# A causal convolution and its experts: from two groups of four batches to four interleaved groups of two

## The chip, the cores and the metric

The kernel runs on one core of one Trainium2 chip. The metric is device time in microseconds (us) of one execution. A profiled execution is a further one, taken by the hardware profiler; times of single instructions come from it.

## What is computed

The reference convolves each of 8 batches (5696 positions, 128 channels) causally with a filter `h`, and sends each of the 45,568 resulting rows to one of 8 experts:

```python
Yf = np.fft.rfft(x, n=2 * S, axis=1) * np.fft.rfft(h, n=2 * S, axis=0)[None]
x = np.fft.irfft(Yf, n=2 * S, axis=1)[:, :S, :].reshape(B * S, D)
logits = x @ w_gate + modality_bias[modality_id]
e_idx = np.argmax(logits, axis=1)                   # gate_w: its softmax value
for e in range(8):
    mask = e_idx == e
    out[mask] = gate_w[mask, None] * (np.maximum(x[mask] @ w1[e], 0.0) @ w2[e])
```

`w1[e]` is 128 by 1024 and `w2[e]` is 1024 by 128, in float32.

## The kernel before

The transform is done as matrix products in stages, for a group `g` of four batches, side by side in the free dimension (512 columns).

- **`stage1(g)`** (L154 to L190): 45 steps `q`. Each loads 128 rows of `x`, splits them into a high part (ACT, L173) and a low part (DVE, L174), runs matmuls of the three products high·high, high·low, low·high (L179), and stores two results `z` to DRAM. Group 0 carries the filter's 128 columns too (640 in all). This splitting in two fp32r parts is used throughout the kernel; a plain fp32 matmul is one instruction in the code and two in the trace.
- **`stage23(g)`** (L195 to L290): 64 steps `k`. Each loads a slice of `z`, does two fp32 matmuls into `px` (L263), two products with the filter on DVE (L265), a sum of the two on POOL (L274; where `whole` holds, half on DVE, L271, and half on POOL, L272), the splitting (ACT L280, DVE L233) and the backward matmuls into `pu` (L243 to L245; plain fp32 in L241 where `whole`), and stores `ut` (ACT L246, then SP).
- **`stage4(g)`** (L306 to L432): again 45 steps `q`. Each loads `u`, splits it (ACT L339, DVE L340), finishes the transform (PE L346), transposes (L353) and computes logits (L360, or in bfloat16 pieces L372). After three `q` a chunk of some twenty small DVE operations picks the expert and a row number for every token, and POOL scatters the rows to DRAM into a region of their expert, 128 rows to an indirect DMA (`dispatch`, L301).
- **`Moe`** (L496 to L632): tiles of rows of one expert. A tile loads 512 rows (L511) and, where the expert changes, 1 MB of weights (L519, SP), splits the weights in four pieces (ACT L524, DVE L526), transposes the rows (L533), and takes eight steps `f` of three matmuls up (`gemm1`, L550 to L552), ReLU and splitting (ACT L555, DVE L556), and three matmuls down two steps later (`gemm2`, L572 to L574). `finish` transposes back (L585), scales (DVE L588) and scatters with four indirect DMAs (POOL L591). The tiles come in four levels, as soon as enough rows are routed: 18, 18 and 45 tiles of 512 rows, and 23 of 256 rows with four steps each.

The order of work: `stage1(0)` alone; then `stage23(0)` with `stage1(1)`; then `stage23(1)` with the first 27 steps of `stage4(0)`; then the experts, beside the other 18 steps of `stage4(0)` and all of `stage4(1)`. `run_all` interleaves such generators at fixed rates, and a scheduler then fixes the order of each engine's queue, which the engines run strictly in order. PSUM has eight banks of 512 fp32 columns: in the third stretch three for `px`, two for `pu`, two for `py` and one for the logits; beside the experts `ps4` has two, the logits one, `pxt` (rows transposed in and out) one, `ph` two and `po` two.

## Time and profile before

| | |
|---|---|
| time, median of 3 runs (lowest to highest) | 2391.52 us (2383.88 to 2395.12) |
| the profiled execution | 2400.92 us, its span 2399.1 us |
| mean granted TensorE clock in it | 0.931 |
| PE (matmuls) busy | 2107.9 us, 88% |
| DVE busy | 1759.2 us, 73% |
| ACT busy | 1418.6 us, 59% |
| POOL busy | 1223.6 us, 51% |
| DMA | 357.46 MB, 149 GB/s on average |

PE is TensorE, DVE VectorE, ACT ScalarE, POOL GpSimd and SP SyncE. The profiled execution is 9.4 us above the median of the runs, so a sum made from its rows is carried to a run by taking 9 us off. A busy PE is not PE at its peak: matmuls overlap, and a matmul at half the granted clock is busy twice as long, so work done is counted from starts, not from busy time.

### The profile page before, as it was taken

To read this page: it belongs to the slowest core of one execution; us is meant where nothing else is said; L and a number is where in the kernel's file an instruction comes from. 1 tells how busy PE (TensorE), PEld (TensorE's weight loads), DVE (VectorE), ACT (ScalarE), POOL (GpSimd) and SP (SyncE) were. 2 spreads that over 40 slices of the span, in tenths; PEclk is the share of its full clock that TensorE was granted. 3 is DMA by queue.
4 is the path that set the end of the run, shared out by engine and by line. 5 is a ranking of instruction groups with operands and counts; after the bars stand their busy time and mean duration, and the time that the engine had idled before them with its cause. 6 is when DMAs were issued, how large, how long until landed. Compare 5 with 4: busy or idle time off the path is not lost. (4 is left out here: it accounts for less than half of the span.)

```text
span 2399.1 us, 33712 instructions
## 1 busy us (share of the span) xinstructions
PE 2107.9 (88%) x9752; PEld 1549.5 (65%) x9752; DVE 1759.2 (73%) x2651; ACT 1418.6 (59%) x2560; POOL 1223.6 (51%) x1012
## 2 busy tenths in 40 slices
PE   6788988999889968896877876999999999999897
PEld 5655544445555436674756654688888888888896
DVE  6569999999879956683555644777777777777675
ACT  6657776555545446573655543566666666666675
POOL 2135455655877875525566655533333333333675
PEclk9999999999888878897888977999999999999999
DMA  9989998786767755332334421223112121112421
GB/s 336 334 301 308 303 293 260 228 270 213 214 197 216 215 155 165 97 127 78 110 110 132 133 78 45 84 80 116 44 43 79 45 80 44 44 45 73 137 75 53
DMA packets 195433, 357.46 MB, mean 149 GB/s; under 512 B 32437, under 2 KB 63513, under 8 KB 191408
## 3 DMA queue, kind: packets, MB, share of 16 engines
q1 hardware_dynamic: 150560, 270.52, 35.4%
q0 software_dynamic: 23520, 47.61, 5.9%
q10 hardware_dynamic: 21168, 37.17, 5.2%
q8 instruction: 78, 1.28, 0.2%
q14 instruction: 107, 0.88, 0.1%
HBM read 276.51 MB, written 157.43 MB: 181 GB/s over the span
## 5 line engine op out<-in xcount | busy, mean ns | idle before, releaser
L556 DVE SCALAR_TENSOR_TENSOR hl<-ph,hh 128x512 fp32r<-128x512 f32 x740 | 509.1, 689 | 325.5 <-ACT hh L555 264.6
L555 ACT ACTIVATE hh<-ph 128x512 fp32r<-128x512 f32 x740 | 444.0, 601 | 443.4 <-PE ph L552 346.8
L591 POOL DMA_INDIRECT out<-of,mrt x370 | 393.9, 1065 | 599.2 <-DVE of L588 470.5
L301 POOL DMA_INDIRECT rows<-rt,idx x360 | 404.7, 1124 | 182.5 <-issue 94.2
L572 PE MATMUL po<-hh,slot 128*128 128x512 f32 (+1 forms) x832 | 331.9, 399 | 41.6 <-issue 25.3
L550 PE MATMUL ph<-mxh,slot 128*128 128x512 f32 (+1 forms) x832 | 327.5, 394 | 19.1 <-DVE hl L556 14.7
L274 POOL TENSOR_TENSOR t<-t,t 96x1024 f32<-96x1024 f32 x90 | 251.9, 2806 | 162.8 <-DVE t L265 142.3
L552 PE MATMUL ph<-mxh,slot 128*128 128x512 f32 (+1 forms) x832 | 315.4, 380 | 1.6 <-issue 0.8
L573 PE MATMUL po<-hl,slot 128*128 128x512 f32 (+1 forms) x832 | 314.2, 378 | 0.1
L551 PE MATMUL ph<-mxl,slot 128*128 128x512 f32 (+1 forms) x832 | 314.3, 378 | 0.0
L574 PE MATMUL po<-hh,slot 128*128 128x512 f32 (+1 forms) x832 | 313.8, 377 | 0.0
L265 DVE TENSOR_TENSOR t<-px,hs 96x1024 f32<-96x1024 f32 x256 | 302.8, 1209 | 13.5 <-PE px L263 6.0
L263 PE MATMUL px<-z,m 96*96 96x512 f32 x512 | 275.9, 632 | 25.9 <-DVE t L265 22.2
L526 DVE TENSOR_TENSOR slot<-raw,slot 128x512 fp32r<-128x512 f32 x370 | 265.4, 720 | 10.9 <-ACT slot L524 10.0
L524 ACT CAST slot<-raw 128x512 fp32r<-128x512 f32 x416 | 251.7, 614 | 11.8 <-DMA raw<-in_w 11.8
L572 PEld LDWEIGHTS po<-hh,slot 128*128 128x128 f32 x832 | 160.4, 193 | 73.0 <-issue 29.0
L550 PEld LDWEIGHTS ph<-mxh,slot 128*128 128x128 f32 x832 | 161.5, 194 | 51.5 <-DVE hl L556 23.9
L246 ACT COPY ut<-pu 90x512 f32<-90x512 f32 x256 | 144.5, 582 | 80.0 <-PE pu L245 27.4
L340 DVE TENSOR_TENSOR ul<-u,uh 128x1024 fp32r<-128x1024 f32 x90 | 117.3, 1304 | 97.6 <-ACT uh L339 75.1
L552 PEld LDWEIGHTS ph<-mxh,slot 128*128 128x128 f32 x832 | 160.6, 193 | 33.6 <-issue 1.4
L573 PEld LDWEIGHTS po<-hl,slot 128*128 128x128 f32 x832 | 160.5, 193 | 31.8 <-issue 1.2
L574 PEld LDWEIGHTS po<-hh,slot 128*128 128x128 f32 x832 | 160.5, 193 | 30.3
(155 smaller groups left out, 3639.7 us busy)
## 6 DMA issues: line engine op xcount, KB each, us to landing
raw<-in_w SPq DMA_DIRECT2D x104, 1024.0 KB
z<-z SPq DMA_DIRECT2D x256, 180.0 KB
z<-z SPq DMA_DIRECT2D x90, 320.0 KB
z<-z SPq DMA_DIRECT2D x90, 256.0 KB
ua<-ut SPq DMA_DIRECT2D x128, 180.0 KB
ub<-ut SPq DMA_DIRECT2D x128, 180.0 KB
mrt<-rows SPq DMA_DIRECT2D x81, 260.0 KB
u<-ua ACTq DMA_DIRECT2D x63, 256.0 KB
```

Of the source, the lines that this page charges most:

```text
L263: nc.tensor.matmul(px[:KP], mm, zbuf[i][k % NZ], start=True, stop=True)
L265: nc.vector.tensor_tensor(prod[i].rearrange("p j (b d) -> p j b d", d=D), px[:KP].rearrange("p (b d) -> p b d", d=D).unsqueeze(1).to_broad ...
L301: nc.gpsimd.indirect_dma_start(views[count[0] % NVIEW], bass.IndirectOffsetOnAxis(ap=idx[:, t:t + 1], axis=0), rt[:, t, :], None, bounds_c ...
L550: nc.tensor.matmul(po, w[:, 0, 0, fs], st["xh"], start=True, stop=False)
L551: nc.tensor.matmul(po, w[:, 0, 0, fs], st["xl"], start=False, stop=False)
L552: nc.tensor.matmul(po, w[:, 0, 1, fs], st["xh"], start=False, stop=True)
L555: st["act"] = nc.scalar.activation(hh, ph, AF.Relu)
L556: nc.vector.scalar_tensor_tensor(hl, ph, 0.0, hh.bitcast(F32), op0=ALU.max, op1=ALU.subtract)
L572: nc.tensor.matmul(po, w[:, 1, 0, fs], hh[:, cs], start=k == 0, stop=False)
L573: nc.tensor.matmul(po, w[:, 1, 0, fs], hl[:, cs], start=False, stop=False)
L574: nc.tensor.matmul(po, w[:, 1, 1, fs], hh[:, cs], start=False, stop=k == 7)
L591: nc.gpsimd.indirect_dma_start(oviews[(t * NSUB + c) % NVIEW], bass.IndirectOffsetOnAxis(ap=ri[:, c, D + 1:D + 2], axis=0), of[:, c, :], N ...
```

## The change

The batches are taken in four groups of two. A group's tiles are 256 columns wide, and where two results stood in two banks, they now share one (`[128, 2, 256]`), so most copies to SBUF keep 512 columns. Counts of the parts that are done per group double: 4 x 45 steps of `stage1` and of `stage4` and 4 x 64 of `stage23`, each of half the width; `stage4` does two `q` together where it copies. Other edits:

- The order of work: `stage1` of group 0 alone; `stage23(0)` with `stage1(1)`; `stage23(1)` with `stage4(0)` and `stage1(2)`; then the experts, beside `stage4(1)` to `stage4(3)`, `stage23(2)`, `stage23(3)` and `stage1(3)`, at the rates `R4`, `R2` and `R1`. There are five levels: 14, 22, 22 and 23 tiles of 512 rows and 23 of 256.
- A `ring` of four PSUM banks (tile name `pb`) serves `stage1`, `px` and `pu` of the later groups, `stage4` and the experts' transposes. `po` has one bank instead of two; at step 2 of a tile no `gemm2` stands, at step 3 two.
- `stage23` splits every `k`; the sum `t` is on POOL (L285), for group 1 at even `k` on DVE. The logits are plain fp32 throughout.
- Stores of `z` (but for group 0) and of `ut` are issued by ACT; loads of `u` by SP.
- Weights are loaded in halves of 512 KB into one buffer each, less far ahead, and compared with the tile before (it was the tile before that); rows are loaded two tiles ahead (it was three).
- The bias goes through DRAM, the twiddle tables are loaded anew by every group, and the filter is reloaded with its negated third part.

The diff, cut to its core:

```diff
-NG = 2
+NG = 4
...
+LAG = 2
+R4 = {1: 0.95, 2: 0.55, 3: 0.6}
+R2, R1 = 0.6, 0.42
+DEPTH = 2
...
-    live = [[g, float(r), 0.0] for g, r in gens]
+    live = [[g, r if callable(r) else lambda r=r: r, 0.0] for g, r in gens]
     while live:
         for it in list(live):
-            it[2] += it[1]
+            it[2] += it[1]()
...
+            for g in range(NG):
+                nc.sync.dma_start(bd[g].rearrange("p (q b) e -> p q b e", b=GB),
+                                  bias.rearrange("p (q b) e -> p q b e", b=B)[:, :, g * GB:(g + 1) * GB])
...
+    def transform(g, q, ft, xx, ps, w):
+
+        for t in range(2):
+            for i, (a, b) in enumerate(((0, 0), (0, 1), (1, 0))):
+                nc.tensor.matmul(ps[:, t, :w], ft[:, a, 2 * t:2 * t + 2, :], xx[:, b], start=i == 0, stop=i == 2)
...
+                ps = ring.tile([128, 2, GC], F32, name="pb")
+                transform(g, q, ft[:, j], xx[:, :, j], ps, GC)
+                z = sp.tile([128, 2, GC], F32, name="z")
+                nc.scalar.copy(z, ps)
+                nc.scalar.dma_start(zd[g][2 * q:2 * q + 2].rearrange("e k t c -> (e k) (t c)"), z.rearrange("p t c -> p (t c)"))
+                yield
+        done.add((1, g))
...
+            pu = ring.tile([128, 2, GC], F32, name="pb")
+            for i in range(2):
+                nc.tensor.matmul(pu[:KP, i], mi[:, i, 0, :], yh[:, i], start=True, stop=False)
+                nc.tensor.matmul(pu[:KP, i], mi[:, i, 0, :], yl[:, i], start=False, stop=False)
+                nc.tensor.matmul(pu[:KP, i], mi[:, i, 1, :], yh[:, i], start=False, stop=True)
+            ut = sp.tile([90, 2, GC], F32, name="ut")
+            nc.scalar.copy(ut, pu[:90])
+            nc.scalar.dma_start(ud[g][:, k], ut)
...
-                px = psx.tile([128, 512], F32, name="px")
-                prod[i] = sp.tile([KP, 2, GC], F32, name=f"t{i}", bufs=4 if i else 5)
-                nc.tensor.matmul(px[:KP], mm, zbuf[i][k % NZ], start=True, stop=True)
+            px = pxp[0].tile([128, 2, GC], F32, name="pb")
+            for h, mm in ((0, m2), (1, m1)):
+                nc.tensor.matmul(px[:KP, h], mm, zbuf[k % NZ][:, 1 - h], start=True, stop=True)
+
+            yv = sp.tile([KP, 2, 2, GC], F32, name="t", bufs=3)
...
-            whole = (g == 1 or k >= W0) and k % WH == WH - 1
-            if whole:
-                nc.vector.tensor_tensor(y[:, 0], y[:, 0], prod[1][:, 0], op=ALU.add)
-                add = nc.gpsimd.tensor_tensor(y[:, 1], y[:, 1], prod[1][:, 1], op=ALU.add)
-            else:
-                add = nc.gpsimd.tensor_tensor(y, y, prod[1], op=ALU.add)
-            with tc.issue_after(add.ins):
-                dispatch(PACE)
-            yh = None
-            if not whole:
-                yh = sp.tile([KP, 2, GC], F32R, name="yh", bufs=4)
-                nc.scalar.copy(yh, y)
+            eng = nc.vector if dve_sum and k % dve_sum == 0 else nc.gpsimd
+            eng.tensor_tensor(yv[:, 0], yv[:, 0], yv[:, 1], op=ALU.add)
+            yh = sp.tile([KP, 2, GC], F32R, name="yh", bufs=3)
+            nc.scalar.copy(yh, yv[:, 0])
...
-            self.raw = [wp.tile([128, 2, FF], F32, name=f"raw{i}") for i in range(NSLOT)]
-            self.slots = [wp.tile([128, 2, 2, FF], F32R, name=f"slot{i}") for i in range(3)]
+        def __init__(self, wp, sp, psh, pso):
+            self.sp, self.psh, self.pso = sp, psh, pso
...
-            nc.sync.dma_start(self.raw[t % NSLOT], w12_d[bass.ds(ex, 1)].rearrange("o p a f -> (o p) a f"), cond=ch > 0)
+            nc.sync.dma_start(self.raw[i], w12_d[bass.ds(ex, 1), :, i].rearrange("o p f -> (o p) f"), cond=ch > 0)
...
-            steps = []
+            for t in range(DEPTH):
+                self.load(t)
+            self.load_weights(0, 0)
+            self.load_weights(0, 1)
+            for k in range(4):
+                self.split(0, k)
+            self.load_weights(1, 0)
...
+                    if f == 0:
+                        while not self.ready(t + DEPTH):
+                            yield
+                        self.load(t + DEPTH)
+                        self.load_weights(t + 1, 1)
+                    if f == n // 2:
+                        self.load_weights(t + 2, 0)
                     self.gemm1(t, f)
-                if g >= LAG:
-                    self.gemm2(*steps[g - LAG][:2])
-                if t + 1 < total:
-                    if n == 4 or f % 2 == 1:
-                        with tc.issue_after(self.st[t]["act"].ins):
-                            self.split(t + 1, f * 4 // n)
-                    if f == (4 if n == 8 else 1):
-                        self.prep(t + 1)
-                if f == LAG and t >= 1:
-                    self.finish(t - 1)
+                    due.append((t, f))
+                    if f == 3 and t >= 1:
+                        self.finish(t - 1)
+
+                    for _ in range(0 if f == 2 else 2 if f == 3 else len(due) > LAG):
+                        self.gemm2(*due.pop(0))
+                    if t + 1 < total:
+                        if n == 4 or f % 2 == 1:
+                            with tc.issue_after(self.st[t]["act"].ins):
+                                self.split(t + 1, f * 4 // n)
+                        if f == (4 if n == 8 else 1):
+                            self.prep(t + 1)
+                    yield
...
+    ring = ctx.enter_context(tc.tile_pool(name="ring", bufs=4, space=PSUM))
+    psl = ctx.enter_context(tc.tile_pool(name="psl", bufs=1, space=PSUM))
...
+            run_all((stage23(0, sp2, pxp, 0, hzp), 1), (stage1(1, sp1), 0.7))
...
+        run_all((stage23(1, sp2, pxp, 2), 1), (stage4(0, sp4, plt), 1.3), (stage1(2, sp1), 0.7), (pace(), 1))
...
+        pxp[0] = ring
...
+        def routing():
+            for g in range(1, NG):
+                rate["4"] = R4[g]
+                while (2, g) not in done:
+                    yield
+                yield from stage4(g, sp4, plt)
+                if g < NG - 1:
+                    fence()
+                    level(g, views[NVIEW])
...
+        def transforms():
+            for g in range(2, NG):
+                while (1, g) not in done:
+                    yield
+                yield from stage23(g, sp2, pxp)
+
+        def pace():
+            while "routing" not in done:
+                dispatch(1)
+                yield
+        run_all((routing(), lambda: rate.get("4", 1)), (transforms(), R2), (stage1(3, sp1), R1), (pace(), 1), (moe.run(), 1))
```

Where instructions now stand. The first place is on PE in the stretch where experts and transforms run together. Before, between `gemm1` (`ph`) and `gemm2` (`po`) steps stand matmuls of `stage4`, here six for one `q` (`py`):

```order
L346 MATMUL py<-uh,gt 128x512
L346 MATMUL py<-ul,gt 128x512
L346 MATMUL py<-uh,gt 128x512 x2
L346 MATMUL py<-ul,gt 128x512
L346 MATMUL py<-uh,gt 128x512
L572 MATMUL po<-hh,slot_7684 128x512
L550 MATMUL ph<-mxh,slot_7685 128x512
L551 MATMUL ph<-mxl,slot_7685 128x512
L552 MATMUL ph<-mxh,slot_7685 128x512
L573 MATMUL po<-hl,slot_7684 128x512
L574 MATMUL po<-hh,slot_7684 128x512
```

Now, at about the 140th of 832 steps of the experts, the same queue holds `stage4` (`pl`, and `pb` from `uu`), `stage23` (`pb` from `zb` and from `yh`) and a tile's transposes (`pb` from `mrt`):

```order
L583 MATMUL po<-hh,slot_7039 128x512
L544 MATMUL pb<-ident,mrt 128x128 x4
L276 MATMUL pb<-zb_78,m_59 96x256
L561 MATMUL ph<-mxh,slot_7038 128x512
L562 MATMUL ph<-mxl,slot_7038 128x512
L563 MATMUL ph<-mxh,slot_7038 128x512
L584 MATMUL po<-hl,slot_7039 128x512
L585 MATMUL po<-hh,slot_7039 128x512
L276 MATMUL pb<-zb_78,m_58 96x256
L257 MATMUL pb<-yh,mi 96x256
L583 MATMUL po<-hh,slot_7039 128x512
```

Three kinds of work from three groups stand between two steps of the experts, and all the tiles named `pb` take turns on the same four banks.

The second place is POOL beside it. Before, only the scatter of rows (`rows`), of results (`out`) and a small copy stand there:

```order
L591 DMA out<-of,mrt 45568x128 x4
L301 DMA rows<-rt,idx 369152x130 x12
L591 DMA out<-of,mrt 45568x128 x4
L301 DMA rows<-rt,idx 369152x130 x8
L327 COPY rt<-tokid 128x12
L301 DMA rows<-rt,idx 369152x130 x2
L591 DMA out<-of,mrt 45568x128 x4
L301 DMA rows<-rt,idx 369152x130 x10
L327 COPY rt<-tokid 128x12
```

Now the sums of `stage23` (`t`) stand between them:

```order
L602 DMA out<-of,mrt 45568x128 x4
L285 TENSOR_TENSOR t<-t 96x512 x2
L310 DMA rows<-rt,idx 369152x130 x12
L357 COPY rt<-tokid 128x4
L310 DMA rows<-rt,idx 369152x130
L285 TENSOR_TENSOR t<-t 96x512
L310 DMA rows<-rt,idx 369152x130 x2
L285 TENSOR_TENSOR t<-t 96x512
L310 DMA rows<-rt,idx 369152x130
L357 COPY rt<-tokid 128x4
```

A run of twelve scatters still stands as one piece, with sums behind it.

The third place is PE at a tile's start in the stretch with experts alone. Before, steps up (L550 to L552) and down (L572 to L574) alternate there; `slot` is the weights:

```order
L572 MATMUL po<-hh,slot_7685 128x512
L550 MATMUL ph<-mxh,slot_7685 128x512
L551 MATMUL ph<-mxl,slot_7685 128x512
L552 MATMUL ph<-mxh,slot_7685 128x512
L573 MATMUL po<-hl,slot_7685 128x512
L574 MATMUL po<-hh,slot_7685 128x512
L572 MATMUL po<-hh,slot_7685 128x512
L550 MATMUL ph<-mxh,slot_7686 128x512
L551 MATMUL ph<-mxl,slot_7686 128x512
```

Now the step numbered 2 has no step down behind it, and two follow the transposes (L596):

```order
L584 MATMUL po<-hl,slot_7039 128x512
L585 MATMUL po<-hh,slot_7039 128x512
L561 MATMUL ph<-mxh,slot_7036 128x512
L562 MATMUL ph<-mxl,slot_7036 128x512
L563 MATMUL ph<-mxh,slot_7036 128x512
L561 MATMUL ph<-mxh,slot_7036 128x512
L562 MATMUL ph<-mxl,slot_7036 128x512
L563 MATMUL ph<-mxh,slot_7036 128x512
L596 MATMUL pb<-ident,ot 128x128 x4
L583 MATMUL po<-hh,slot_7037 128x512
L584 MATMUL po<-hl,slot_7037 128x512
L585 MATMUL po<-hh,slot_7037 128x512
```

Two steps up stand side by side, which hold both banks of `ph`.

572 lines of the change are left out of this document (267 added, 305 removed).

## The prediction

> **What bounds the kernel now.** I read the page first, then the busy times by stretch, cut where one part of the program gives way to the next, and last single rows for the prices.
>
> ```profile
> span 2399.1 us, 33712 instructions
> PE 2107.9 (88%) x9752; PEld 1549.5 (65%) x9752; DVE 1759.2 (73%) x2651; ACT 1418.6 (59%) x2560; POOL 1223.6 (51%) x1012
> ```
>
> PE is the fullest engine, but 88% is an average over stretches with different limits:
>
> ```profile
> core 0: us, PE busy (x) PEld busy (x) DVE busy (x) ACT busy (x) POOL busy (x), PEclk, DMA share, GB/s
> 0.00:145.00 145.00, 98.49 (x541) 85.68 (x541) 88.29 (x105) 87.07 (x127) 19.49 (x45) 0.95 0.95 339
> 145.00:480.00 335.00, 299.26 (x985) 165.36 (x986) 312.77 (x241) 232.66 (x425) 190.87 (x91) 0.97 0.87 276
> 480.00:905.00 425.00, 367.71 (x1315) 205.25 (x1314) 354.42 (x461) 216.78 (x381) 306.48 (x215) 0.88 0.69 210
> 905.00:1530.00 625.00, 501.37 (x2539) 389.87 (x2537) 365.30 (x802) 331.60 (x607) 349.02 (x337) 0.86 0.34 107
> 1530.00:2210.00 680.00, 678.88 (x3129) 549.05 (x3129) 512.68 (x851) 430.31 (x782) 238.08 (x226) 1.00 0.20 63
> 2210.00:2399.00 189.00, 162.16 (x1249) 154.25 (x1247) 125.75 (x194) 120.22 (x239) 119.64 (x100) 0.96 0.28 91
> ```
>
> The first transform (to 145) is bound by DMA, 95% busy. Its second stage (to 480) is bound by DVE, 93%. To 905 DVE is fullest again, but at 83%. From 905 to 1530 experts and routing share the engines and nothing is full: PE 80%, and that at a granted clock of 0.86. From 1530 experts run alone with PE at 100% and clock 1.00, and the small tiles at the end reach 86%. So about 900 us pass before PE has its main work, and 625 more in which it is fed badly; the change addresses both.
>
> PE's true work I count from starts, where matmuls stand densely:
>
> ```profile
> 704.59 0.63 PE L346 MATMUL py<-uh,gt 128*128 128x512 f32 x1
> 705.01 1.91 PE L263 MATMUL px<-z,m 96*96 96x512 f32 x2
> 705.93 1.42 PE L346 MATMUL py<-uh,gt 128*128 128x512 f32 x1
> ...
> 1273.00 1.84 PE L360 MATMUL pl<-wg,yt 128*128 128x8 f32 x16
> 1274.70 0.47 PE L550 MATMUL ph<-mxh,slot 128*128 128x512 f32 x1
> ...
> 1809.62 0.39 PE L550 MATMUL ph<-mxh,slot 128*128 128x512 f32 x1
> 1809.85 0.40 PE L551 MATMUL ph<-mxl,slot 128*128 128x512 f32 x1
> ```
>
> From start to start, an fp32r matmul of 512 columns takes 0.23 us, one plain fp32 matmul of 512 (two records) 0.92, a pair of logit records 0.23. A tile of the experts has 48 matmuls and 8 transposes; 3129 in 680 us make 56 in 12.1 us, 1.51 us for each of eight steps.
>
> **The change part by part.** The matmuls keep their columns: twice as many of half the width. I take their time as halved, so 0.46 for fp32 and 0.117 for fp32r of 256. What changes is when they can run. Prices for the other engines:
>
> ```profile
> L265 DVE TENSOR_TENSOR t<-px,hs 96x1024 f32<-96x1024 f32 x256 | 302.8, 1209 | 13.5 <-PE px L263 6.0 <-DMA z<-z 3.9 <-ACT hs L227 1.4
> L526 DVE TENSOR_TENSOR slot<-raw,slot 128x512 fp32r<-128x512 f32 x370 | 265.4, 720 | 10.9 <-ACT slot L524 10.0 <-issue 0.8
> L272 POOL TENSOR_TENSOR t<-t,t 96x512 f32<-96x512 f32 x38 | 57.0, 1501 | 31.9 <-DVE t L265 23.7 <-DVE idx L420 4.1 <-ACT ut L246 2.7
> L588 DVE TENSOR_TENSOR of<-pxt,mrt 128x512 f32<-128x512 f32 x81 | 55.1, 680 | 16.0 <-remote 8.7 <-PE py L346 5.6 <-PE pxt L585 0.9
> L301 POOL DMA_INDIRECT rows<-rt,idx x360 | 404.7, 1124 | 182.5 <-issue 94.2 <-ACT slot L524 29.2 <-DVE hl L556 18.1
> L591 POOL DMA_INDIRECT out<-of,mrt x370 | 393.9, 1065 | 599.2 <-DVE of L588 470.5 <-issue 85.5 <-DVE lg L389 12.6
> L556 DVE SCALAR_TENSOR_TENSOR hl<-ph,hh 128x512 fp32r<-128x512 f32 x740 | 509.1, 689 | 325.5 <-ACT hh L555 264.6 <-issue 45.3 <-ACT yt L356 7.5
> L555 ACT ACTIVATE hh<-ph 128x512 fp32r<-128x512 f32 x740 | 444.0, 601 | 443.4 <-PE ph L552 346.8 <-remote 45.1 <-issue 22.5
> L414 DVE TENSOR_TENSOR pos<-pos,oh 128x96 f32<-128x96 f32 x30 | 16.2, 540 | 0.0
> L413 DVE TENSOR_TENSOR base<-pl,base 128x8 f32<-128x8 f32 x30 | 4.6, 153 | 0.0
> ```
>
> The last two are the largest and the smallest of fifteen groups that make a routing chunk, 117 us over 30 chunks, so some 4 us each.
>
> *The first transform* moves 45 x (320 + 640) KB now and 45 x (192 + 384) KB after:
>
> ```profile
> z<-z SPq DMA_DIRECT2D x90, 320.0 KB
> xt<-in_xq SPq DMA_DIRECT2D x45, 320.0 KB
> q0 software_dynamic: 23520, 47.61, 5.9%
> ```
>
> 17.7 MB less at 339 GB/s is 52 us: 93. The bias's way to DRAM adds 23,040 pieces of 64 bytes, which no row shows. They cost at least nothing; at most, at the price of q0's 23,520 much larger packets (5.9% of 16 engines' span), 142 us. I take 22, near the lower end because they are 1.5 MB. 115 us.
>
> *stage23(0) with stage1(1)* is half as wide. DVE's product falls from 1209 ns to about 680 (the nearest row with a PSUM input and 512 columns, L588), so the work is 0.56 of 335, 188 us. The stored filter grows by a half, 3 MB, 12 us at 276 GB/s: 200.
>
> *stage23(1) with stage4(0) and stage1(2)*, DVE: 128 products x 0.68 = 87, 64 low parts and 45 of `u` x 0.72 = 78, 32 sums = 22, six chunks x 4 = 24, low parts of `x` and tables 40: 251 us. At the 83% that DVE reaches in 480:905, 302. Storing from ACT's queue I take at nothing: ACT has 217 of 425 busy there, and the copy and the store are apart in its order. If that cover is gone, ACT waits at each of 391 stores for its copy, up to 0.6 us.
>
> ```profile
> L550 PE MATMUL ph<-mxh,slot x832: 277/397/797, 917.2 to 2383.7; 128*128 128x512 f32 x130, 128*128 128x256 f32 x37
> ```
>
> With 12 us from the start of the experts' part to their first matmul, as now (905 to 917), that matmul comes at 630 instead of 917.
>
> *Experts beside the rest.* By the order, stage4(1) ends at the experts' step 90, stage4(2) at 252, stage4(3) at 388 of 832. One group of `stage4` is 270 matmuls x 0.117, 90 transposes x 0.11 and 90 logits x 0.23, 63 us of PE. A `k` of `stage23` is 0.92 + 0.70; a `q` of `stage1` 0.70.
>
> - M1 (to step 90): 63 + 53 x 0.92 + 49 x 0.70 + 45 x 0.70 + 90 x 1.51 = 314 us.
> - M2 (to 252): 63 + 75 x 0.92 + 79 x 0.70 + 162 x 1.51 = 432.
> - M3 (to 388): 63 + 136 x 1.51 = 268.
>
> DVE in the same three: a step of the experts costs 1.13 us (513 of 680 busy, 8 steps in 12.1), a `k` 2 x 0.68 + 0.72, a `stage4` group 67, `stage1` 26: 305, 406, 221. POOL: a scatter of rows 1.39 with its issue, one of results 1.30, a sum 1.50: 264, 342, 213. So PE is fullest in all three, but DVE stands at 97, 94 and 82% of it. An engine this closely accompanied does not reach 100%. I take 0.85, 0.90 and 0.95: 0.83 is what the fullest engine reaches in 480:905, with chains as here, and 1.00 what PE reaches with experts alone, whose steps are the greater part of M3. 369 + 480 + 282 = 1131 us.
>
> The banks speak against this. The four of the ring are taken in turn by six kinds of tiles, where 905:1530 had three for its two kinds; a slow reader of one stops PE for all. The granted clock shows what gaps on PE do: 0.86 in 905:1530, 1.00 where PE is fed. The Trainium skill, TensorE: Matmul & The Clock Gate, "A second HAM failure mode: psum-queue depth-cycling", says that a PE which idles briefly between groups while cycling through PSUM banks drops to its slow clock again and again. At a clock of 0.86 throughout, the three would take 1014 / 0.86 = 1179 us instead of 1131, and the total would be 48 us higher. The trace has the low clock, but not yet with a ring.
>
> *The tail.* 260 steps of large tiles alone, 393 us. At step 3 PE meets both `ph` banks taken: ACT's ReLU, 0.60, and DVE's 0.69 must follow the step before last, and 1.4 us of matmuls stand between instead of 2.1. I take 0.3 us a tile, 10 in all. The small tiles take 177 us now (189 less the one large tile that 1249 matmuls leave beside 23 x 52). Their weights now come in halves, asked for two steps of some 1.5 us ahead:
>
> ```profile
> 2252.76 4.84 DMA raw<-in_w
> ...
> 2314.74 4.99 DMA raw<-in_w
> ```
>
> Even the present kernel, asking two tiles ahead, waits 5 us for them twice on the chain. I add 10. The tail is 590.
>
> Sum: 630 + 1131 + 590 = 2351 for the span, 2353 with the 1.8 us around it. The profiled execution (2400.9) is 9.4 above the median: **2344**, 2.0% below 2391.5.
>
> **The rivals.**
>
> *DVE becomes the bound (slower).* In M1 and M2, 128 sums on POOL run beside DVE's splits:
>
> ```profile
> L174 DVE TENSOR_TENSOR xl<-xt,xh x90: 673/826/2890, 5.8 to 382.0; 128x640 fp32r<-128x640 f32 x45, 128x512 fp32r<-128x512 f32 x45
> L233 DVE TENSOR_TENSOR yl<-t,yh x90: 1202/1211/4941, 166.0 to 862.8; 96x1024 fp32r<-96x1024 f32 x90
> ```
>
> ```profile
> L233 DVE TENSOR_TENSOR yl<-t,yh 96x1024 fp32r<-96x1024 f32 x90 | 160.1, 1779 | 17.9 <-ACT yh L280 5.9 <-PE px L263 5.8 <-PE pu L244 4.1
> L274 POOL TENSOR_TENSOR t<-t,t 96x1024 f32<-96x1024 f32 x90 | 251.9, 2806 | 162.8 <-DVE t L265 142.3
> ```
>
> The medians are the plain price, the longest a whole POOL sum (2.8 us) or more above it. I put it at 0.12 us for each of the some 410 splits (`yl`, whose 160 us over 90 is 568 ns above its median, scaled by the sums' length, 1.5 against 2.8 us, and by POOL's share for sums, 0.22 in M1 against 0.57 in 145:480): DVE 328 and 433, more than PE's 314 and 432. With DVE at 0.80, the share that the fullest engine has in 905:1530, the two take 410 + 541, and M3 at 0.90 298: 1249, 118 more, 2462. It decides once DVE's rate in M1 and M2 is under 0.85, where the gain is used up. For it: PE, DVE and POOL all carry 79% or more of the largest load here, and even the less crowded 905:1530 left PE idle for a fifth. Against it: experts' steps are always at hand. The Trainium skill, SBUF — State Buffer, "SBUF: two separate sides", calls the ports shared by DVE and POOL an exclusive lock, held for the whole instruction, when DVE has two SBUF inputs; by the longest durations above, the trace agrees.
>
> *The weights eat the gain (same).* If each of some eight changes of expert in the last level, and as many among the large tiles alone, waits for both halves at 2 to 3 us, that is 32 x 2.5 less the 10 counted and some 25 that large tiles hide, 45 us: 2389. The two waits of 5 us speak for it; against it, most loads find the expert unchanged.
>
> *The engines fit as well as with experts alone (better).* M1 to M3 at 0.95 throughout: 1067 us, 64 less; with nothing for bias and tail, 42 less again: 2238. For it: M3-like work already runs at 1.00. Against it: no stretch with transforms does.
>
> **How the numbers follow.** Forecast 0.42, better 0.10, same 0.13, DVE bound 0.35. About 0.5%, 12 us, is what a measurement of this kernel can tell from no change. Faster: 0.52; same: 0.13; slower: 0.35. Cases of both signs hold most of the chance; the forecast's own range is 2300 to 2379 (rates 0.03 up or down, bias 0 to 40). The whole range, 2240 to 2490, leaves out half of the better case and the worst third of the slower one, 0.17; the bias's upper end of 142 falls inside it.
>
> **What would show it.** In the new profile the experts' first matmul should start near 630, stage4(3)'s last near 1760, and large tiles alone should take 12.4 us each. Between 630 and 1760 PE should be busy over 90% at a granted clock above 0.92. If DVE is busier than PE there, or `yl` and `slot` take well over 0.8 us on average, the DVE rival is right; if PE waits for tiles named `pb`, the ring is the limit. A first matmul after 700 would mean that the prices of the first three stretches were wrong; a tail over 620, those of the weights.

## The result, and the profile after

The changed kernel takes **2496.7 us** (median of 4 runs, 2488.58 to 2502.18), the kernel before 2387.7 beside it (4 runs): a ratio of 1.0451, 95% interval 1.0407 to 1.0495. It is slower, outside the forecast's range of 2240 to 2490 by 7 us and 153 us from the forecast itself. The page of the profiled execution (2494.9 us):

```profile
span 2493.2 us, 40599 instructions
PE 2127.2 (85%) x11732; PEld 1770.0 (71%) x11732; DVE 1813.2 (73%) x3288; ACT 1557.8 (62%) x3158; POOL 1206.7 (48%) x1147
```

The busy times by stretch, cut at the new parts' borders: first transform, `stage23(0)`, `stage23(1)`, then M1, M2 and M3 of the prediction, large tiles alone, small tiles:

```profile
core 0: us, PE busy (x) PEld busy (x) DVE busy (x) ACT busy (x) POOL busy (x), PEclk, DMA share, GB/s
0.00:115.00 115.00, 66.76 (x267) 56.50 (x268) 61.45 (x114) 61.40 (x123) 20.79 (x60) 0.81 0.93 270
115.00:320.00 205.00, 177.16 (x1026) 141.84 (x1024) 169.29 (x241) 152.62 (x325) 98.14 (x64) 0.96 0.92 295
320.00:635.00 315.00, 232.51 (x1491) 204.58 (x1491) 240.71 (x495) 206.18 (x451) 158.56 (x146) 0.83 0.79 249
635.00:1000.00 365.00, 334.22 (x1926) 281.67 (x1926) 296.24 (x520) 255.94 (x540) 214.35 (x193) 0.95 0.65 198
1000.00:1525.00 525.00, 468.24 (x2514) 384.03 (x2513) 416.07 (x746) 318.56 (x635) 300.79 (x272) 0.93 0.50 149
1525.00:1900.00 375.00, 300.31 (x1536) 244.18 (x1534) 217.14 (x479) 204.33 (x418) 171.77 (x182) 0.88 0.29 90
1900.00:2310.00 410.00, 390.36 (x1750) 307.21 (x1750) 297.73 (x511) 243.99 (x439) 129.00 (x133) 0.98 0.19 58
2310.00:2493.00 183.00, 157.59 (x1231) 150.03 (x1229) 114.55 (x189) 114.81 (x233) 113.36 (x100) 0.96 0.20 60
```

Up to 635 it goes as forecast, and M1 too: PE 92% at a clock of 0.95. Then it falls off: M2 has 0.93, and M3, which I took for the easiest of the three, has PE at 80% and 0.88 with no other engine over 58%. The experts' matmuls by their source line:

```profile
L561 PE MATMUL ph<-mxh,slot x832: 274/393/796, 634.6 to 2477.7; 128*128 128x512 f32 x130, 128*128 128x256 f32 x37
```

First matmul 634.6 (forecast 630). From the starts of steps 0, 90, 252 and 388: M1 359 (forecast 369), M2 528 (480), M3 369 (282), the tail 602 (590). The sum is missed by 142 us, 135 of it in M2 and M3.

What ACT waited for in M3, then what ACT and POOL did around one such wait:

```profile
ACT hh L566 <- PE ph L563: 53.0, 59, 3.0
ACT rt L373 <- remote: 47.4, 5, 15.0
ACT hh L566 <- remote: 23.8, 4, 13.7
```

```profile
1603.97 0.59 ACT L379 COPY yt<-pb 128x512 f32<-128x512 f32 x1 [2.26 <-PE ph L563]
1619.51 0.59 ACT L373 COPY rt<-pb 128x512 f32<-128x512 f32 x1 [14.96 <-remote]
1620.00 0.60 ACT L566 ACTIVATE hh<-ph 128x512 fp32r<-128x512 f32 x1
```

```profile
1591.04 0.97 POOL L310 DMA_INDIRECT rows<-rt,idx  x1 [9.19 <-ACT hh L566]
1592.32 0.97 POOL L310 DMA_INDIRECT rows<-rt,idx  x1 [0.30 <-issue]
...
1602.76 0.97 POOL L602 DMA_INDIRECT out<-of,mrt  x1 [0.30 <-issue]
...
1615.61 0.97 POOL L310 DMA_INDIRECT rows<-rt,idx  x1 [0.31 <-issue]
1616.57 0.21 POOL L357 COPY rt<-tokid 128x4 int32<-128x4 int32 x1
```

The copy at L373 stands still for 15 us. The instructions that it waits for by its program had all ended: the scatters that last read its buffer by 1539, the token copy into it at 1543, its last matmul at 1600. It goes on 3 us after a run of 20 indirect DMAs, 1.28 us apart, and PE, DVE and ACT all stand meanwhile. I call this a **hold**: idle time of ACT or DVE after the last instruction that its waits name had ended, if over 2.5 us. Added up over the stretch where experts run beside the rest, holds are 113 us here. The kernel before has them too, 146 us between 905 and 1540: the "remote 45.1" in the quoted row of its L555, which I had read past, is a part of them. The sums are rough: no view lists holds, each wait has to be matched with the program, and a stricter count of waits that a DMA's landing may have ended gives 108 and 104.

### The profile page after: what moved, and what is told of

Its sections match the earlier page's. It is cut to its first block, busy times and chain, and to the rows that moved or that the text cites. A ratio compares the mean times of both kernels' runs of the same rounds, so it can differ in the third digit from the quotient of the medians.

```text
span 2493.2 us, 40599 instructions
## 1 busy us (share of the span) xinstructions
PE 2127.2 (85%) x11732; PEld 1770.0 (71%) x11732; DVE 1813.2 (73%) x3288; ACT 1557.8 (62%) x3158; POOL 1206.7 (48%) x1147
## 4 chain that ended last, share of the span: by engine, by line
PE 32%; issue 5%; DVE 4%; ACT 4%; another core or an unknown queue 3%; DMA 2%; POOL 1%; SPq 1%; POOLq 0%; ACTq 0%; DVEq 0%
PE ph L561 4%; PE po L583 4%; PE ph L563 4%; PE ph L562 4%; PE po L585 4%; PE po L584 4%; PE pb L370 2%; ACT hh L566 2%; DVE hl L567 2%; PE pb L596 1%; PE pb L544 1%; PE pb L276 1%; PE pl L382 1%; DMA raw<-in_w 1%
## 5 line engine op out<-in xcount | busy, mean ns | idle before, releaser
L285 POOL TENSOR_TENSOR t<-t 96x512 f32<-96x512 f32 x224 | 332.4, 1490 | 445.7 <-DVE t L281 348.9
L281 DVE TENSOR_TENSOR t<-pb,hs 96x512 f32<-96x512 f32 x512 | 325.7, 677 | 39.2 <-PE pb L276 13.5
L276 PE MATMUL pb<-zb,m 96*96 96x256 f32 x1024 | 280.4, 399 | 23.3 <-DMA zb<-z 15.4
L251 DVE TENSOR_TENSOR yl<-t,yh 96x512 fp32r<-96x512 f32 x256 | 210.3, 824 | 58.6 <-ACT yh L287 27.4
L561 PEld LDWEIGHTS ph<-mxh,slot 128*128 128x128 f32 x832 | 161.5, 195 | 98.8 <-DVE hl L567 64.6
L583 PEld LDWEIGHTS po<-hh,slot 128*128 128x128 f32 x832 | 162.0, 195 | 97.2 <-ACT hh L566 53.2
L287 ACT CAST yh<-t 96x512 fp32r<-96x512 f32 x256 | 157.7, 619 | 99.9 <-POOL t L285 91.7
L276 PEld LDWEIGHTS pb<-zb,m 96*96 96x96 f32 x1024 | 164.0, 171 | 68.5 <-DVE t L281 10.0
L257 PE MATMUL pb<-yh,mi 96*96 96x256 f32 x512 | 170.9, 334 | 38.7 <-ACT yh L287 17.5
L261 ACT COPY ut<-pb 90x512 f32<-90x512 f32 x256 | 148.4, 581 | 59.9 <-DMA u<-ut 26.4
```

What stands on the lines that cost most here:

```text
L276: nc.tensor.matmul(px[:KP, h], mm, zbuf[k % NZ][:, 1 - h], start=True, stop=True)
L285: eng.tensor_tensor(yv[:, 0], yv[:, 0], yv[:, 1], op=ALU.add)
L561: nc.tensor.matmul(po, w[:, 0, fs], st["xh"], start=True, stop=False)
L583: nc.tensor.matmul(po, w[:, 0, fs], hh[:, cs], start=k == 0, stop=False)
```

## The experiments

Theories at the outset: **holds** (runs of indirect DMAs on POOL stop ACT and DVE, and the change has more of them), **DVE** (the prediction's rival, with the port lock), **ring** (four banks for six kinds of tiles), **start gap** (PE idle ahead of the first expert matmul). The kernels ran on several chips, and the kernel before takes 2384 to 2409 us on some and 2278 on others; so each ratio is against the kernel before on the same chip. The sums of holds are good to some 10 to 50 us.

| kernel | us | ratio to before (interval) | M1, M2, M3 | holds |
|---|---|---|---|---|
| before, after (first result) | 2387.7, 2496.7 | 1.0451 (1.0407 to 1.0495) | 359, 528, 369 | 146, 113 |
| e1 token copy on DVE | 2501.29 | 1.0398 (1.0320 to 1.0477) | 356, 532, 375 | 144 |
| e2 scatters behind sums | 2488.70 | 1.0334 (1.0244 to 1.0423) | 347, 519, 375 | 125 |
| e3 half the sums on DVE | 2519.49 | 1.0492 (1.0402 to 1.0582) | 355, 542, 375 | 167 |
| e5 experts 14 rounds later | 2547.00 | 1.0586 (1.0506 to 1.0666) | 391, 523, 366 | 186 |
| e7 ring of 3, `po` of 2 | 2514.67 | 1.0539 (1.0481 to 1.0597) | 386, 526, 380 | 155 |
| e8 fillers between scatters | 2753.05 | 1.1549 (1.1487 to 1.1611) | 413, 563, 430 | 0 |
| e10 scatters paced | 2454.13 | 1.0298 (1.0237 to 1.0358) | 348, 537, 327 | 82 |
| e13 paced and aged | 2388.52 | 1.0480 (1.0437 to 1.0523) | 348, 504, 295 | 18 |
| e14 less DVE work | 2388.85 | 1.0467 (1.0429 to 1.0505) | 343, 507, 298 | 9 |
| e17 earlier routing | 2403.54 | 1.0538 (1.0498 to 1.0578) | 358, 504, 294 | 5 |
| b2 before, paced | 2292.59 | 1.0064 (1.0041 to 1.0086) | | 5 |
| c1 after again | 2506.25 | 1.0461 (1.0401 to 1.0521) | 359, 530, 374 | 127 |
| c3 before, paced | 2349.18 | 0.9795 (0.9738 to 0.9853) | | 54 |
| c4 after, paced as e13 | 2442.98 | 1.0199 (1.0139 to 1.0260) | 347, 518, 329 | 74 |
| c5 after, third chip | 2400.65 | 1.0550 (1.0515 to 1.0585) | 360, 506, 292 | 8 |

e1 to e5 shared one chip (the kernel before 2408.7 there); e7 to e12 and c1 to c4 a second (2383.9 and 2397.2); e13, e14, e17 and b2 a third (2278.5); c5 and c6 a fourth (2278.0). The chip of the first result is not on record.

### Which of the four

**e1_tok_dve** takes from POOL the copy that ACT's L373 waits for.

```diff
-                nc.gpsimd.tensor_copy(rt[:, :n * GB, D + 1:].bitcast(I32).rearrange("p (q b) o -> p q (b o)", b=GB),
+                nc.vector.tensor_copy(rt[:, :n * GB, D + 1:].bitcast(I32).rearrange("p (q b) o -> p q (b o)", b=GB),
```

> One word changed: the copy of the token numbers into rt (L357) is given to DVE instead of POOL. POOL's-queue theory: the third stretch (steps 252 to 388), 369 us, loses the stalls of ACT in front of L373 and L566 (15.0, 13.5, 12.2, 4.4 and 13.7 us, 59 in all) and comes to 310 to 330; the stretches before it gain 0 to 15; in all 2430 to 2455. DVE-bound theory: DVE gets 92 more copies, so no gain, 2490 to 2510. Four-banks theory: no change, 2490 to 2505. If the token copy has only taken the blame and the routing chain itself is late, ACT's stalls of 12 to 15 us stay, under another name.

Holds 144 us, M3 375: the copy is not what ACT stands for.

**e2_spread** puts each scatter of rows behind the last sum or scatter of results, so that they mix on POOL.

```diff
+                if last[0] is None:
+                    dispatch(1)
+                else:
+                    with tc.issue_after(last[0].ins):
+                        dispatch(1)
```

> In the part with the experts each scatter of rows is tied behind POOL's latest sum or output scatter, so that runs of 8 to 12 scatters become runs of 1 to 3 between sums. POOL's-queue theory: sums (L285) no longer stand behind a burst of 10 to 15 us, ACT's waits for them (29 and 51 us in the first two stretches) halve, the second stretch falls from 528 to 495 to 515, and the third, where token copies also come free, by 20 to 50; in all 2430 to 2470. DVE-bound and four-banks theories: within 10 us of 2497. Against: rows land later, so a table may be later; then the waits on the fence grow and it is slower than 2500.

M1 and M2 are 9 and 13 us shorter than in e1 on the same chip, M3, which has no sums to stand between, is the same (375). That fits runs of DMAs as the cause, but the gain is small, and the intervals of the two ratios overlap.

**e3_dve_sums** gives DVE every second sum of groups 2 and 3.

```diff
-                yield from stage23(g, sp2, pxp)
+                yield from stage23(g, sp2, pxp, 2)
```

> Every second sum (L285) of the third and fourth groups' transforms goes to DVE (64 of 128; 0.81 us each there, against 1.31 us on POOL). DVE-bound theory: DVE gets 64 x 0.81 = 52 us and loses some 20 of stretched yl and slot, so 30 us more in the first two stretches, 2520 to 2540; if the stretched instructions are the whole loss, their means fall from 0.84 and 0.83 to near 0.75 and the two stretches gain 20. POOL's-queue theory: 84 us less on POOL, ACT's waits for sums fall by a third or more, and the first two stretches (360 + 528) gain 15 to 40, the third nothing; 2455 to 2485. Four-banks theory: no change.

M2 is 542, 14 us above the first profile's; M1 355. More DVE work bought nothing and, in the ratio, cost nothing that the intervals separate.

**e5_fill** starts the experts' part 14 rounds later, to fill the start gap with transforms.

```diff
+        def later(gen, n):
+            for _ in range(n):
+                yield
+            yield from gen
...
-        run_all((routing(), lambda: rate.get("4", 1)), (transforms(), R2), (stage1(3, sp1), R1), (pace(), 1), (moe.run(), 1))
+        run_all((routing(), lambda: rate.get("4", 1)), (transforms(), R2), (stage1(3, sp1), R1), (pace(), 1), (later(moe.run(), 14), 1))
```

> The experts' steps start 14 rounds of the interleaving later, so that in program order transforms of later groups stand ahead of them. POOL's-queue theory: the 38 us in which PE waits for the first rows, while POOL works off some 30 scatters, are filled with transforms that would else be done between later steps; PE idle before the first expert matmul falls to under 10 us and 20 to 35 us are gained in all, 2460 to 2480. If the sums of those transforms stand behind the same scatters on POOL, the fill stops after the first few and the gain is under 10. The other theories say nothing of it.

The first matmul comes at 663.1, 28 us later, and M1 is not shorter but 391: a loss.

### Holds by themselves

**e7_ring3** moves one bank from the ring to `po`.

```diff
-    ring = ctx.enter_context(tc.tile_pool(name="ring", bufs=4, space=PSUM))
+    ring = ctx.enter_context(tc.tile_pool(name="ring", bufs=3, space=PSUM))
...
-            tc.tile_pool(name="pm2", bufs=1, space=PSUM) as pso, tc.manual_schedule(engines={mybir.EngineType.SP}):
+            tc.tile_pool(name="pm2", bufs=2, space=PSUM) as pso, tc.manual_schedule(engines={mybir.EngineType.SP}):
```

> Three shared PSUM banks instead of four, and two banks for the second product instead of one. Four-banks theory: with one bank fewer the first two stretches (360 and 528) grow by 20 or more each and so does the part ahead of the experts, 2540 or more; the last part (12.5 us for a large tile) falls to 12.2 if the single bank of the second product was its loss. If the shared banks are not short, nothing moves by more than 10 us. Burst and queue theories: no change.

Against c1, the unaltered changed kernel on this chip, M1 is 27 us longer (386 against 359), M2 and M3 are the same within 6, and the large tiles alone take 411 instead of 426. Both changes count in M1, M2 and M3, so the bank by itself is not priced there; with a second for `po`, giving it up costs 27 us in M1 and nothing later. The second `po` bank is worth 15 us where large tiles are alone: they take 12.0 us each instead of 12.6.

**e8_space** puts four small additions on POOL behind each scatter of the experts' part (added work on a scratch tile).

```diff
+                    gap = last[0]
+                    for _ in range(4):
+                        with tc.issue_after(gap.ins):
+                            gap = nc.gpsimd.tensor_tensor(scratch, ident, ident, op=ALU.add)
```

> In the part with the experts, four small additions on POOL (128 x 128, no use for the result) stand after each scatter of rows, so that scatters are no longer back to back; POOL's runs get longer. Burst theory: the whole-core stalls of the third stretch (five, 53 us in all) go, and it falls from 369 to 310 to 335; the stretches before get 0 to 30 longer, since sums stand behind the additions; in all 2450 to 2480. Queue theory: runs that take twice as long stall twice as long, the third stretch grows by 20 to 50, in all 2530 or more.

Without long runs no hold is left, but the kernel is the slowest of all. POOL is late with the rows, and SP, waiting for them, keeps everything behind it. ACT's longest wait, 55 to 140 us into M3, and PE's, later:

```profile
ACT slot L536 <- DMA raw<-in_w: 73.2, 4, 69.7
```

```profile
PE pb L545 <- DMA mrt<-rows: 92.6, 1, 92.6
```

**e10_paced** has each scatter wait for the newest `hh` through a one-column copy on POOL, so that scatters go out at the pace of the experts' steps.

```diff
+                if queue and moe.hh is not None:
+                    hold = nc.gpsimd.tensor_copy(pin, moe.hh[:, 0:1].bitcast(F32))
+                    with tc.issue_after(hold.ins):
+                        dispatch(1)
```

> In the part with the experts each scatter of rows has to wait for the newest activation of the experts (a copy of one column on POOL reads it first), so that about one scatter goes out for each step and not 12 to 16 in one run. Burst theory: the third stretch loses most of its 53 us of whole-core stalls, 369 to 315 to 335, the second some 10 to 20; in all 2430 to 2460. Queue theory: what stands behind a scatter waits no longer than a step, so a gain of the same kind; but if the scatters are now late for the tables, the waits on rows grow and it is slower. This run tells whether pacing is worth it, the one with additions tells why.

1.0298 against 1.0461 for the unaltered kernel on this chip (c1): 39 us won. M3 is 47 us shorter, M2 7 longer. Holds go from 127 to 82 us; of those over 6 us two are left.

**e12_probe** adds, in the tail, bursts of 4, 8, 16, 16 and 12 scatters into a buffer that nobody reads, at tiles 55, 59, 63, 67 and 71.

```diff
+                    if f == 0 and t in BURST:
+                        hold = nc.gpsimd.tensor_copy(dummy, st_h(self, t, f))
+                        for _ in range(BURST[t]):
...
+                                hold = nc.gpsimd.indirect_dma_start(
```

> Scatters that nobody waits for: while only large experts' tiles run, POOL gets extra indirect DMAs of 128 rows into a buffer that is no longer read, 4 with tile 55, 8 with 59, 16 with 63 and with 67, 12 with 71; beside the tiles' own 4 output scatters that makes unbroken runs of up to 20. Burst theory (an unbroken run of more than some ten of POOL's indirect DMAs holds up the other engines even where nothing depends on it): no stall at 4 and 8, and at the runs of 16 to 20 all of PE, ACT and DVE stand still for 5 to 14 us, about 20 to 35 us in all. Queue theory (only what stands behind the run on POOL or waits for its data is late): the tiles go on, except that output scatters are late by up to 20 us, and of and mrt have room for that: 0 to 10 us in all.

One run, 2521.97 us. Tiles take 12.6 us; after 4 scatters none is longer, after 8 one takes 16.8, after 16 two take 15.7 and 20.4, again 14.3 and 23.5, after 12 14.3 and 17.8: 35 us in all. ACT and DVE stand for 24 us more than in the same tail without bursts. Some 11 of these are two waits of ACT for weights, the rest four holds of 2.9 to 3.7 us, one at each burst of 8 or more. But most of the delay runs through queues: results stand behind the burst on POOL, SP's loads of rows wait for a buffer until those have gone, and the weights stand behind those loads. So a burst of 8 to 16 scatters makes at most a small hold here; the 15 us of M3 are not reproduced, and what more they need is not shown.

### Another chip

**e13_aged** paces as e10, and lets a scatter go at the earliest four rounds after its row number is known.

```diff
+                credit = min(credit + (1.2 if rate.get("4", 1) > 0.9 else 1.0), 2.0)
+                while credit >= 1.0 and queue and r - stamp[0] >= 4:
...
+                    hold = nc.gpsimd.tensor_copy(pin, moe.hh[:, 0:1].bitcast(F32))
```

> As the paced run, and a scatter goes out at the earliest four rounds after its chunk's places are known, so that the runs of 7 and 8 that were left break up too (1.2 scatters a round in the first stretch, else 1). Burst theory (a long unbroken run of POOL's indirect DMAs holds up ACT and with it the core, though no wait of the program is open): the paced run's 2454 falls by another 5 to 20, and no whole-core stall over 4 us is left between 660 and 1900. Queue theory alone (only what really waits for late data is late): rows are later by four rounds, so no gain, 2450 to 2480.

M3 295 and 18 us of holds, as hoped; but the kernel before takes 2278.5 here, 105 to 130 us less than on the chips so far, and the ratio is 1.048. That was the surprise that needed settling: this chip has next to no holds at all (e17, not paced, has 5 us).

**e14_nodve** leaves out the low halves of the weights in tiles 2 to 47, 184 subtractions of 0.73 us on DVE.

```diff
+            if 2 <= t < 48:
+                return
```

> Leaves work out: the low halves of the weights are not made for tiles 2 to 47 (184 subtractions on DVE, 0.69 to 0.83 us each, some 135 us of DVE; the matmuls use what stands in the buffer). DVE-bound theory: the first two stretches (360 and 528, DVE 81% and 79% busy) lose what DVE is spared there, 25 and 55 us, in all 2400 to 2430. Burst theory: DVE is not what is waited for, 2475 to 2495, and the third stretch stays near 369. If PE comes out less idle but at a lower clock, the gain is partly eaten, 2440 to 2470.

M2 by windows here, and of e17, whose DVE work is whole:

```profile
989.00:1495.00 506.00, 462.21 (x2516) 381.76 (x2515) 370.31 (x656) 320.10 (x637) 289.95 (x272) 0.95 0.52 156
```

```profile
997.00:1501.00 504.00, 462.53 (x2521) 381.57 (x2521) 418.61 (x742) 319.35 (x638) 304.38 (x276) 0.95 0.52 156
```

DVE is busy 48 us less, and M2 lasts as long. The bound of M2 is not DVE. M1, where DVE also has less to do, is 15 us shorter (343 against 358), though it also began 8 us later; there DVE's work may count.

**e17_early** runs `stage4(0)` faster, so that its last rows are routed sooner.

```diff
-        run_all((stage23(1, sp2, pxp, 2), 1), (stage4(0, sp4, plt), 1.3), (stage1(2, sp1), 0.7), (pace(), 1))
+        run_all((stage23(1, sp2, pxp, 2), 1), (stage4(0, sp4, plt), 1.55), (stage1(2, sp1), 0.7), (pace(), 1))
```

> Routing of the first group runs at 1.55 steps a round instead of 1.3 beside the second group's transforms, so that its last scatters go out while transforms still run. If the 39 us of idle PE ahead of the first expert matmul are the run of some 26 scatters and nothing else, they fall to 5 to 20 and the kernel gains as much, 2465 to 2485. If POOL's sums of the transforms are pushed back by the scatters, the gain is given back before the start, 2490 to 2505.

PE's wait for the first rows falls from 38 to 11 us, and the first matmul still comes at 638: the time went into the stretch before.

**b2_paced** and, later, **c3_before_paced** are the kernel before, with its scatters paced alike.

```diff
-            while not paced and queue:
-                dispatch(4)
-                yield
...
+                    while credit >= 1.0 and queue and r - stamp[0] >= 3 and moe.hh is not None:
...
+                        hold = nc.gpsimd.tensor_copy(pin, moe.hh[:, 0:1].bitcast(F32))
...
-            run_all((rest(), RATE), (moe.run(), 1))
+            run_all((rest(), 0.83), (pace(), 1), (moe.run(), 1))
```

> The kernel before, with its scatters beside the experts paced in the same way (one for each expert step, three rounds after its chunk at the earliest, routing at 0.83 steps a round because its own scatter steps are gone) instead of four at a time in one run. Burst theory: between 905 and 1530 ACT or DVE stood for 146 us in waits that the program doesn't explain; if half of it was on the path, 2390 falls to 2310 to 2350. Queue theory alone: within 20 us of 2390.

1.0064 on the chip without holds: pacing costs 14 us where there is nothing to pace.

### The same kernels on both kinds of chip

On the chip with holds, the changed kernel and the kernel before unaltered, and both paced:

> The changed kernel as it is, on the same chip as the kernel before. If the holds (waits of ACT and DVE that nothing in the program explains) are no part of the difference, the ratio is 1.04 to 1.055 on any chip, and the changed kernel takes 2375 to 2400 where the kernel before takes 2280, 2490 to 2510 where that takes 2390. If the holds are what made it slower, the ratio is 0.99 to 1.02 on a chip without them. On a chip without holds the stretches from the first expert matmul (steps 0 to 90, 90 to 252, 252 to 388) should be near 357, 504 and 294, and 360, 528 and 369 on one with them.

> The kernel before, for its profile on this chip. With holds, the stretch from 905 to 1530 is some 625 us long and ACT and DVE stand 146 us without a reason in the program; without holds it is 510 to 540 long, with under 20 such us, and the rest of the kernel is as long as it was.

> The kernel before with paced scatters again (1.0064 of the kernel before on the fourth chip). On a chip with holds pacing removes most of them: 0.95 to 0.98 of the kernel before, faster than both kernels. On a chip without holds 1.00 to 1.01 as before. If it is 1.00 to 1.01 on a chip with holds as well, the holds were never on the path of the kernel before.

> The changed kernel with paced and delayed scatters again (1.048 of the kernel before on the fourth chip). On a chip with holds 1.015 to 1.03 of the kernel before, 40 to 70 us under the changed kernel as it is; on a chip without holds within 10 us of it.

Unaltered 2506.25 and 2389.72 (one run, 175 us of holds), paced 2442.98 and **2349.18**. The last, at 0.9795 (0.9738 to 0.9853), beats both kernels there. M3 of c1, then of c4, where pacing takes 45 us out of it with PE's instructions the same:

```profile
1525.00:1899.00 374.00, 296.29 (x1512) 239.44 (x1512) 211.47 (x457) 200.66 (x410) 165.83 (x178) 0.88 0.29 90
```

```profile
1502.00:1831.00 329.00, 290.68 (x1512) 235.41 (x1510) 210.51 (x455) 198.45 (x410) 183.38 (x251) 0.95 0.33 102
```

On a fourth chip both kernels unaltered:

> The changed kernel as it is. If the holds are no part of the difference: 1.04 to 1.055 of the kernel before, with or without holds on this chip; without them the stretches of the experts' steps 0 to 90, 90 to 252, 252 to 388 are near 357, 504 and 294 us. If the holds made it slower: 0.99 to 1.02 on a chip without them.

> The kernel before, for its profile on the same chip. Without holds 2270 to 2290 us and under 20 us in which ACT and DVE stand without a reason in the program; with them 2380 to 2410 and 140 to 180 such us.

The changed kernel 2400.65, ratio 1.055 (1.0515 to 1.0585); the kernel before 2277.99 (c6, one run, 2267.85). Holds are 8 and 17 us. Here the two can be compared without them. The windows of before (c6), then of after (c5):

```profile
0.00:145.00 145.00, 102.50 (x540) 89.34 (x540) 87.05 (x104) 86.62 (x127) 19.62 (x45) 0.92 0.94 333
145.00:480.00 335.00, 297.34 (x982) 165.69 (x982) 307.60 (x241) 231.38 (x423) 190.19 (x90) 0.97 0.87 278
480.00:895.00 415.00, 373.88 (x1373) 209.80 (x1371) 367.67 (x480) 221.29 (x391) 309.88 (x213) 0.90 0.71 219
895.00:1410.00 515.00, 468.15 (x2547) 376.92 (x2547) 370.30 (x821) 331.82 (x611) 357.84 (x344) 0.95 0.41 127
1410.00:2078.00 668.00, 663.81 (x3062) 538.11 (x3063) 499.78 (x812) 422.13 (x769) 231.82 (x222) 0.99 0.20 63
2078.00:2266.00 188.00, 162.74 (x1254) 154.66 (x1252) 124.21 (x195) 121.09 (x240) 118.69 (x100) 0.96 0.28 92
```

```profile
0.00:115.00 115.00, 64.76 (x270) 54.80 (x270) 62.64 (x115) 61.91 (x125) 20.70 (x60) 0.84 0.93 273
115.00:320.00 205.00, 176.01 (x1027) 140.67 (x1028) 169.16 (x241) 155.05 (x328) 99.72 (x64) 0.97 0.93 296
320.00:640.00 320.00, 229.84 (x1497) 202.27 (x1498) 242.38 (x501) 207.53 (x453) 162.60 (x146) 0.84 0.77 246
640.00:1000.00 360.00, 334.05 (x1913) 285.73 (x1912) 292.98 (x516) 253.54 (x533) 217.45 (x193) 0.93 0.64 198
1000.00:1500.00 500.00, 457.91 (x2507) 379.10 (x2506) 420.99 (x738) 316.74 (x633) 299.35 (x270) 0.96 0.52 155
1500.00:1800.00 300.00, 286.49 (x1544) 235.27 (x1543) 220.40 (x488) 205.32 (x421) 170.04 (x180) 0.99 0.38 114
1800.00:2215.00 415.00, 390.18 (x1761) 307.06 (x1762) 298.63 (x510) 244.58 (x440) 134.10 (x137) 0.98 0.19 58
2215.00:2396.00 181.00, 155.34 (x1219) 148.06 (x1217) 114.42 (x187) 113.69 (x231) 111.49 (x98) 0.97 0.20 60
```

Busy time times granted clock is taken as PE's work at full clock, and what it leaves of a stretch is lost (515 - 468.15 x 0.95 = 70 us in 895:1410). PE's work is the same in both kernels, 1977 and 1985 us; lost are 289 and 411. The clock is given to 0.01, so a part is good to some 10 us. By parts:

| lost, us | before | after | |
|---|---|---|---|
| ahead of the experts | 176 in 895 us | 222 in 640 us | +46 |
| experts beside the rest | 70 in 515 | 126 in 1160 | +56 |
| experts alone, small tiles | 43 in 856 | 63 in 596 | +20 |

By the same working, the first two profiles lose 426 and 525 us, 137 and 114 more than these: about their 146 and 113 us of holds.

## Why the prediction was wrong

**The step that failed** is the reading of the stretch from 905 to 1530: "625 more in which it is fed badly; the change addresses both". It lost 194 us there (625 - 501.37 x 0.86). On a chip without holds the same work (2547 matmuls, 2539 there) takes 515 us and loses 70. So some 124 of the 194 us went with the holds, and the change keeps what goes with them, the long runs of scatters on POOL. I had priced the changed kernel by rates without holds and compared it with a time that has 146 us of them; what looked like the gain was that difference. With the changed kernel's own 113 us added, the sum of 2351 becomes 2464, against a span of 2493.2. In the terms of the sum, it is the rates of M2 and M3 that were too high: 0.90 and 0.95 were put, and 432 us of work in 528 and 268 in 369 make 0.82 and 0.73, where the same kernel on a chip without holds reaches 0.88 and 0.95.

**Holds are not why the change is slower.** The ratio is 1.045 and 1.046 on chips that have them, 1.055 on one that has not. Without them the change loses its 123 us in three other places, here in the times and the work of c6 and c5:

- *Ahead of the experts*: 255 us less (895 to 640), for 301 us of PE's work that left (719 to 418, time less loss). The losses stayed: the first transform loses 61 instead of 51, and there is a start gap. I took 12 us from the start of the experts' part to its first matmul, "as now". PE waits 38 us there, in the first profile and in c5 alike, while POOL works off 26 scatters in one run that stand ahead of the fence:

```profile
PE pb L544 <- DMA mrt<-rows: 38.4, 1, 38.4
```

The first matmul came at 634.6 nevertheless, since the stretch before was shorter than my 302 by about as much (272, to PE's last matmul at 592). That the start came out right was luck: two errors cancelled. e5 and e17 moved the gap and won nothing.

- *Experts beside the rest*: 645 us more (515 to 1160), for 589 us of work, 301 of it from the stretches ahead and 280 from the experts alone. PE's share at full clock rises from 0.863 to 0.891 there, but the experts alone had 0.98: what the transforms gain from the company, the experts' steps lose.
- *Experts alone and small tiles*: 260 us less (856 to 596), for 280 of work. Large tiles take 12.6 us where I had 12.4, 12.1 before, some 16 us over 31 tiles. I had put the 0.3 us on both `ph` banks being taken; but e7, which leaves those alone and gives `po` its second bank back, takes 12.0, so it is the one `po` bank. And tile 50 takes 33 in c5, where the kernel before has no such tile. SP stands at L700, where the pad rows wait for the last scatters, and the next tile's rows are loaded behind it. SP's wait and PE's there:

```profile
SPq L700 <- DMA rows<-rt,idx: 21.0, 4, 13.4
```

```profile
PE pb L544 <- DMA mrt<-rows: 15.0, 1, 15.0
```

The prediction named no queue for this step. By the tiles this makes some 35 us, where the table has 20: its parts are rough. The three make 645 - 255 - 260 = 130 us, the difference of the two spans. Had the work that left freed time at the rates of where it was, 0.80 and 0.98, that would be 375 + 285 = 660 us against 645: even then a gain of 15 only. By the forecast's own sum, 2351, the changed kernel was never faster than a kernel before without holds, 2266; a sum priced without holds was set against a time with them.

**What held.** The work in M1, M2 and M3: 314, 432 and 268 us forecast, 311, 440 and 284 by c5's windows. The rates on a chip without holds: 0.85, 0.90 and 0.95 forecast, 0.86, 0.88 and 0.95 measured. The small tiles, 187 forecast, took 177 and their weights cost nothing to speak of. By steps, M2 was 506 for 480 and M3 292 for 282, the large tiles 428 for 403, M1 359 for 369. In sum 2396 against 2351, 2% below.

**The rivals.** The one with DVE as the bound gave the nearest time, 2462, for a wrong reason: PE stays busier than DVE in M1, M2 and M3, and e14 takes 48 us from DVE in M2 without shortening it. In M1 it may have a part, up to 15 us by e14. (In 480:905 of the kernel before, too, PE was busier, 368 us against DVE's 354, and not DVE, as I read it; DVE was fullest only against PE's work at full clock.) What it rests on is there. The plain price of `yl` and `slot` is unchanged, the longest ones are not:

```profile
L251 DVE TENSOR_TENSOR yl<-t,yh x128: 653/678/2476, 651.9 to 1421.1; 96x512 fp32r<-96x512 f32 x128
L537 DVE TENSOR_TENSOR slot<-raw,slot x130: 658/681/3334, 634.6 to 1521.2; 128x512 fp32r<-128x512 f32 x130
```

Their means are 840 and 825 ns (`slot` has 681 where no sums run on POOL), 0.15 us above the medians, near the 0.12 that I put. The ring costs little as far as tried: one bank fewer, with a second for `po`, is 27 us in M1 and nothing later; more than four banks were not run. The sign that I named for it, PE waiting for `pb`, stands for some 20 us each in M1 and M2 of c5, and more than half of it is for an operand (`yh`, `zb`) and not for a bank. The largest such row in each:

```profile
PE pb L257 <- ACT yh L287: 13.3, 7, 4.1
```

```profile
PE pb L257 <- ACT yh L287: 9.4, 6, 3.4
```

The rule of the Trainium skill that was weighed against it (TensorE: Matmul & The Clock Gate, "A second HAM failure mode: psum-queue depth-cycling") would have PE drop to its slow clock in the mixed stretches. The runs give it little room: without holds the granted clock there is 0.93, 0.96 and 0.99, higher than the 0.86 of the first profile of before, whose low clock came with the holds (0.95 in c6). "Weights eat the gain" and "the engines fit better" did not happen.

**What is open.** Why a hold lasts until some 3 us after the run of DMAs, and why two chips have them and two have not, no run shows. That holds go with long unbroken runs of scatters (14 to 30 beside those that I looked at) is shown by e10 and c4 against c1, by c3 against c2, and by the chips; e12's bursts alone made only small ones. The trace's semaphore events narrow it. In the first profile of after, ACT and DVE have 20 waits over 1 us, 114 us in all, that the profile calls "remote" (21 and 111 us in c1, none in c5 and c6), and each ended on an update of the semaphore that PE raises, recorded up to 16 us after PE's last instruction that raises it. In the wait shown above, PE started nothing between 1604.61 and 1620.65, yet three of its updates are recorded between 1619.45 and 1619.57, and ACT goes on at 1619.51; POOL's signal of 1616.79 came in time. So what is late is PE's signal. Whether its matmuls ended late too (their ends are modelled) or only the signal, and what the scatters have to do with it, is not shown. What part of M2's 26 us over the forecast is chains between engines and what part banks was not separated.

## What to carry to other kernels

Before a badly filled stretch is credited to the order of work, look at how its idle time comes: if it is in pieces of 10 us and more with a releaser that the profile can't name ("remote"), find out what stands beside them, and ask whether the change touches that. Work that is interleaved fills another's gaps, but pays with its own rate; the gain is the difference of the two, at the rates of the mixed stretch and of each alone. And where chips differ, run both kernels on each kind: a ratio from one chip may hide what its time is made of.
